# Lookups of expert places moved back in TensorE's order: two spacing numbers of a Fourier-filter and expert-routing kernel

## The chip, the cores and the metric

The kernel runs on one core of a Trainium2 chip. The metric is the device time of one execution in microseconds: 1575.86 us, the median of three runs (1575.03 to 1579.9).

## The reference

Two stages, one behind the other. The first filters 8 sequences of 2496 tokens with 256 channels in the frequency domain. The second routes the 19968 filtered tokens to 8 experts. Each expert takes at most 2496 tokens; the pairs of token and expert are taken in falling order of their score, and a pair whose token is placed or whose expert is full is passed over. Each expert is a two-layer network.

```python
X = np.fft.rfft(x, axis=1)
Y = X * (filt_r + 1j * filt_i)[None, :, :]
x = np.fft.irfft(Y, n=x.shape[1], axis=1).reshape(B * S, D)   # 19968 x 256
cap = N // E                                                  # 2496
flat = (x @ w_gate).flatten()
for idx in np.argsort(-flat):
    tok, e = int(idx) // E, int(idx) % E
    if assigned[tok] >= 0 or counts[e] >= cap:
        continue
    assigned[tok] = e
    counts[e] += 1
for e in range(E):
    mask = assigned == e
    out[mask] = np.maximum(x[mask] @ w1[e], 0.0) @ w2[e]
```

## The kernel before

Up to about 515 us the kernel computes the filter as products with small Fourier matrices and writes the filtered tokens to DRAM (`xs`). From there on it works expert by expert. The greedy assignment is not walked through pair by pair: the kernel finds, eight times, the next expert that fills up, by a search over score thresholds. So experts are numbered 0 to 7 in the order in which they fill up, and while TensorE multiplies for expert e, the search for a later one runs beside it.

**Expert products** (`Ffn.run`). An expert's 2496 rows go in five blocks of 512 (the last of 448). The first layer takes 8 groups of 6 products per block (L872, tile `pz`, 512 or 448 columns; each operand is split into a high and a low part, so three terms). ScalarE takes the positive part (L878) and VectorE the low part of that (L886, for the last block L889, both write `hl`). The second layer takes 24 products per 128 rows (L921, tile `py`, 256 columns). Gathered rows are turned on TensorE (L850) and split by ScalarE (L853) and VectorE (L854). Raw weights are split into high and low parts by ScalarE (L829) and VectorE (L830).

**The search** (`Route.phase`, `threshold`, `counts`). Eleven rounds per expert. In each, VectorE writes a 0/1 mask per token and threshold (`Gm`, L572), TensorE counts with 11 or 13 small products over the rank table `A` (L580), VectorE folds that into `X` (L588 to L590), TensorE sums it over the partitions (L593), and VectorE derives the next thresholds (L617 to L632, `thr` at L610). When the last round is done, a prefix product (L720) gives each partition its first place, and the next expert's preparation runs on VectorE: the maximum over the remaining experts (`M`, L657), two passes over `tmp` (L659, L661), `ar` (L663, L664) and the new rank table `A` (L667). The first count of the next search needs this `A`.

**The lookups** (`Route.places`). They turn the settled assignment into row numbers to gather from (`xid`) and to write to (`oid`). The 2496 places of an expert go in five groups of 512. Per group VectorE makes a one-hot table `OH` (L770, L771), and TensorE looks up two times two blocks of 128 places with it (L777, a pair of products into one PSUM tile `rt`). Behind each pair VectorE takes `loc` (L778), ScalarE two sums (L781), VectorE `ex` (L782); behind the second pair `js`, `xid`, `t1b`, `oid` (L785 to L793). So there are ten pairs per expert. GpSimd then gathers the rows (L836) and later scatters the results (L932). The `rt` tiles of lookups, counts, sums and the prefix product share two PSUM buffers in turn: each waits for the readers of the tile two before it.

**What sets the order.** TensorE's order is written out by hand: `emit` runs through the expert products, and each piece of them advances a clock in class `Pump` by its estimated time (0.65 for three first-layer or six second-layer products, about a microsecond in units of 1). The search and the lookups are generators that yield the kind of their next wait and its length; `Pump.feed` takes their next step when the clock is past its due time. For the lookups the length is taken as it stands: `LO[0]` ahead of the first group, `LO[1]` ahead of the first pair of every later group, `LO[2]` ahead of the second pair of each group, and 3.0 behind a group:

```python
yield 'o', LO[0] if ch == 0 else LO[1]      # L772, OH is issued
...
if t == 0:
    yield 'p', LO[2]                        # L784, between the pairs
...
yield 'g', ch                               # L794, xid and oid are issued
```

One lookup step is taken at most per piece of product. The search waits until the first group of the lookups under way is done (`Pump.first`). If a gather needs a group that the clock hasn't reached, `Pump.until` takes the missing steps at once, with no products between. The other engines' orders are set by a scheduler that plays the program through in time when it is built, so they shift with TensorE's. SP's queue carries loads of the first stage only; GpSimd's carries the gathers, scatters and weight loads.

Of the kernel before, what the change touches and what calls it, by code (L numbers as in the profile page):

```python
# [19 lines left out]
NPOST = 6  # L20

LAGS = [(1.6, 1.2), (1.9, 1.2), (2.4, 1.4), (2.2, 1.3), (2.2, 1.2), (2.6, 1.2), (2.6, 1.2), (2.6, 1.2)]
LO, M0, M1, M7 = (4.2, 1.2, 1.4), 3.5, 4.9, 6.9
TU0, TU, PACE = 1.1, 1.15, 5
ORD, TF = (1, 0, 0, 1), (3, 5)
I1, C0, EZ = 5, -2, 0.8
# [1120 lines left out]
```

## Time and profile before

| | |
|---|---|
| median of three runs | 1575.86 us |
| the profiled execution | 1576.41 us |
| its span, first to last instruction | 1574.5 us |
| TensorE busy: products, weight loads | 90%, 79% |
| VectorE, ScalarE, GpSimd busy | 62%, 46%, 36% |
| mean granted TensorE clock | 0.971 of 2.4 GHz |
| prefix products (L720), start | 497.3, 637.8, 767.0, 892.0, 1011.6, 1133.0, 1249.8, 1276.8 us |

Products on TensorE overlap their neighbours, so their rate is read from the distance of starts. A wait is shown as idle time ahead of an instruction, with the one that ended it last. The granted clock has two levels, 1.2 and 2.4 GHz; a share between 0.5 and 1 in a stretch is a mixture of the two.

### The profile page before, as it was taken

Reading aid. Unit: us, or ns where it says so; the run is one execution under the profiler, and the core shown is the slowest. Engines: PE = TensorE matmul, PEld = TensorE weight load, DVE = VectorE, ACT = ScalarE, POOL = GpSimd, SP = SyncE. Lnnn points to the kernel's source line nnn. Section 1 sums busy time; section 2 is a strip of 40 time slices with the busy share of each in tenths; the row PEclk is TensorE's granted clock in tenths of the full one; section 3 lists DMA queues with packets and bytes.
Section 4 is the critical chain, followed back from the end, with each engine's and each line's share of the span. In section 5 each row is a group of like instructions: output and inputs, shape, how many; then the busy total and the mean of one; then the engine's idle time right before and its main releaser. Section 6 shows DMA issues by size and latency. Waiting matters only on the chain.

```text
span 1574.5 us, 27463 instructions
## 1 busy us (share of the span) xinstructions
PE 1416.7 (90%) x10354; PEld 1237.7 (79%) x10354; DVE 983.8 (62%) x2611; ACT 718.8 (46%) x1703; POOL 564.0 (36%) x566
## 2 busy tenths in 40 slices
PE   0478889999899689989999999999999999999998
PEld 0478888886654478878888888888879889899898
DVE  1558878765656646966786686787686772622322
ACT  1455666663356532633552553453462453632322
POOL 0124544432310253354253344343533443333311
PEclk9989999999999789999999999999999999999999
DMA  9998978447889410211221211211211221111100
GB/s 147 159 120 131 131 133 134 99 134 220 237 280 356 130 52 28 84 57 33 78 66 36 75 44 53 76 51 43 92 42 40 93 98 44 45 44 44 44 28 26
DMA packets 117992, 150.61 MB, mean 96 GB/s; under 512 B 72525, under 2 KB 95651, under 8 KB 115555
## 3 DMA queue, kind: packets, MB, share of 16 engines
q1 hardware_dynamic: 70900, 45.23, 17.1%
q0 software_dynamic: 17840, 60.34, 11.8%
q10 hardware_dynamic: 29119, 43.28, 9.4%
q8 instruction: 82, 1.34, 0.4%
q14 instruction: 51, 0.42, 0.1%
HBM read 85.13 MB, written 63.70 MB: 95 GB/s over the span
## 4 chain that ended last, share of the span: by engine, by line
PE 56%; DVE 14%; DMA 12%; issue 8%; ACT 4%; SPq 2%; POOL 2%; ACTq 1%; another core or an unknown queue 0%; POOLq 0%; DVEq 0%
PE py L921 21%; PE pz L872 20%; DMA xt<-x 6%; PE pv L409 4%; DMA zd<-zt 3%; PE rt L580 2%; DVE xr L211 2%; PE ptr L850 2%; PE p L238 2%; PE pa L293 2%; PE p L223 2%; ACT lg L740 1%; DVE hl L886 1%; POOL out L932 1%; DMA wr<-moe_w,widx 1%
## 5 line engine op out<-in xcount | busy, mean ns | idle before, releaser
L921 PE MATMUL py<-w1h,hl 128*128 128x256 f32 x2496 | 485.8, 287 | 2.0 <-DVE hl L889 1.4
L921 PEld LDWEIGHTS py<-w1h,hl 128*128 128x128 f32 x2496 | 403.5, 192 | 5.5 <-DVE hl L889 2.2
L921 PE MATMUL py<-w1l,hl 128*128 128x256 f32 (+1 forms) x1280 | 360.1, 283 | 0.0
L932 POOL DMA_INDIRECT out<-y,oid x160 | 174.3, 1090 | 452.0 <-ACT y L931 411.9
L878 ACT ACTIVATE hl<-pz 128x512 fp32r<-128x512 f32 (+1 forms) x320 | 187.0, 589 | 224.0 <-PE pz L872 183.2
L872 PE MATMUL pz<-xo,w0h 128*128 128x512 f32 (+1 forms) x640 | 266.9, 417 | 12.1 <-DVE hl L886 6.2
L872 PE MATMUL pz<-z,w0h 128*128 128x512 f32 (+1 forms) x640 | 250.4, 391 | 1.5 <-DVE z L854 1.3
L872 PE MATMUL pz<-xo,w0l 128*128 128x512 f32 (+1 forms) x640 | 251.2, 392 | 0.0
L921 PEld LDWEIGHTS py<-w1l,hl 128*128 128x128 f32 (+1 forms) x1280 | 242.5, 189 | 2.0
L886 DVE SCALAR_TENSOR_TENSOR hl<-pz,hl 128x512 fp32r<-128x512 f32 x227 | 154.8, 687 | 126.0 <-ACT hl L878 123.5
L836 POOL DMA_INDIRECT xg<-xs,xid x160 | 171.1, 1069 | 140.2 <-PE ptr L850 45.9
L931 ACT COPY y<-py 128x256 f32<-128x256 f32 x152 | 56.3, 371 | 294.9 <-PE py L921 255.1
L223 PE MATMUL p<-cS,xr 117*128 117x120 f32 x688 | 97.5, 288 | 64.9 <-ACT xr L211 49.1
L872 PEld LDWEIGHTS pz<-xo,w0h 128*128 128x128 f32 x640 | 123.6, 193 | 33.5 <-DVE hl L886 8.5
L223 PEld LDWEIGHTS p<-cS,xr 117*128 117x128 f32 x688 | 88.9, 202 | 70.3 <-ACT xr L211 49.1
L872 PEld LDWEIGHTS pz<-xo,w0l 128*128 128x128 f32 x640 | 122.1, 191 | 24.3
L872 PEld LDWEIGHTS pz<-z,w0h 128*128 128x128 f32 x640 | 123.0, 192 | 18.1 <-DVE z L854 2.6
L231 ACT COPY Y<-p 64x240 f32<-64x240 f32 (+1 forms) x304 | 116.3, 382 | 25.1 <-PE p L223 15.3
L246 POOL TENSOR_TENSOR P<-P 128x256 f32<-128x256 f32 x80 | 62.3, 780 | 162.7 <-DVE P L244 162.6
L572 DVE TENSOR_TENSOR Gm<-M,thr 117x1232 bf16<-117x1232 f32 (+2 forms) x80 | 104.4, 1315 | 0.2
L238 PE MATMUL p<-cW,Y 128*128 128x128 f32 x640 | 91.3, 284 | 10.6 <-DVE Q L245 7.2
L238 PEld LDWEIGHTS p<-cW,Y 128*128 128x128 f32 x640 | 82.3, 197 | 17.1 <-issue 9.1
(230 smaller groups left out, 2260.7 us busy)
## 6 DMA issues: line engine op xcount, KB each, us to landing
zd<-zt ACTq DMA_DIRECT2D x80, 256.0 KB
xt<-x SPq DMA_DIRECT2D x42, 344.0 KB
z<-zd SPq DMA_DIRECT2D x18, 600.0 KB
xs<-xo ACTq DMA_DIRECT2D x18, 600.0 KB
xt<-zd SPq DMA_DIRECT2D x8, 600.0 KB
xs<-xt ACTq DMA_DIRECT2D x8, 600.0 KB
xs<-Y ACTq DMA_DIRECT2D x6, 600.0 KB
xt<-x SPq DMA_DIRECT2D x147, 21.5 KB
```

The lines of the kernel that those rows point to most:

```text
L223: s.lastmm = nc.tensor.matmul(p[:, q-q0, :120], xv[:, q-24*h], s.cS1, start=True, stop=True).ins
L231: (nc.vector.tensor_copy if t in ((5,) if b else (1, 3, 5, 7, 9)) else nc.scalar.copy)(dst, src)
L238: nc.tensor.matmul(p[:, k], s.Y1[b][:, 4*g+k, dh*128:dh*128+128], s.cW[:, 4*g+k], start=True, stop=True)
L246: nc.gpsimd.tensor_tensor(P[:, :, :64], P[:, :, :64], P[:, :, 64:], op=OP.subtract)
L409: nc.tensor.matmul(p[:120, :w], s.cD, z[:, g-g0:g-g0+w], start=True, stop=True)
L572: nc.vector.tensor_tensor(Gm[:, s0:s1, :m], s.M[:, s0:s1].unsqueeze(2).to_broadcast([117, s1 - s0, m]), thr[:117].unsqueeze(1).to_broadcas ...
L836: s.lastg = s.nc.gpsimd.indirect_dma_start(out=xg[:n], out_offset=None, in_=s.xs, in_offset=bass.IndirectOffsetOnAxis(ap=ids[0][:n, t:t+1] ...
L872: nc.tensor.matmul(p[:, :n], w[:, sl], x[:, k, :n], start=m == 0, stop=m == 5)
L878: s.lasta = nc.scalar.activation(h[:, :n], p[:, :n], AF.Relu).ins
L886: nc.vector.scalar_tensor_tensor(l[:, :n], p[:, :n], 0.0, h[:, :n].bitcast(F32), op0=OP.max, op1=OP.subtract)
L921: nc.tensor.matmul(p[:a.stop-a.start], hs[g][f][:, a], b[:, 256*f:256*f+256], start=m == 0, stop=m == 8 * len(terms) - 1, skip_group_check ...
L932: st = nc.gpsimd.indirect_dma_start(out=out_rows, out_offset=bass.IndirectOffsetOnAxis(ap=ids[1][:w, 4*g+t:4*g+t+1], axis=0), in_=y[:w], i ...
```

## The change

`LO[1]` goes from 1.2 to 2.0 and `LO[2]` from 1.4 to 2.2. (`M0`, `M1` and `M7` stay.)

```diff
-LO, M0, M1, M7 = (4.2, 1.2, 1.4), 3.5, 4.9, 6.9
+LO, M0, M1, M7 = (4.2, 2.0, 2.2), 3.5, 4.9, 6.9
```

All instructions stay; TensorE, VectorE, ScalarE and GpSimd get another order, SP keeps its own. From the prefix product to the first count of the next search stood seven pairs of lookups for experts 1 to 3 and eight for 4 and 5; now it is six for each.

On TensorE, ahead of the first count (`Gm`, L580) behind expert 3's lookups. Names are tiles with their buffer numbers, `pz` the first-layer result and `OH` the one-hot table. Before:

```order
L872 MATMUL pz_10495<-xo_10135,w0l_8477 128x448
L777 LDWEIGHTS OH_10480
L777 MATMUL rt_10502<-tab1_3992,OH_10480 128x180
L777 LDWEIGHTS OH_10480
L777 MATMUL rt_10502<-tab1_3992,OH_10480 128x180
L872 MATMUL pz_10513<-xo_10135,w0h_8476 128x448
L872 MATMUL pz_10513<-z_10136,w0h_8476 128x448
L872 MATMUL pz_10513<-xo_10135,w0l_8477 128x448
L872 MATMUL pz_10513<-xo_10135,w0h_8476 128x448
L872 MATMUL pz_10513<-z_10136,w0h_8476 128x448
L872 MATMUL pz_10513<-xo_10135,w0l_8477 128x448
L580 LDWEIGHTS Gm_3966
```

And now:

```order
L872 MATMUL pz_10498<-z_10134,w0h_8476 128x448
L872 MATMUL pz_10498<-xo_10133,w0l_8477 128x448
L872 MATMUL pz_10511<-xo_10133,w0h_8476 128x448
L872 MATMUL pz_10511<-z_10134,w0h_8476 128x448
L872 MATMUL pz_10511<-xo_10133,w0l_8477 128x448
L872 MATMUL pz_10511<-xo_10133,w0h_8476 128x448
L872 MATMUL pz_10511<-z_10134,w0h_8476 128x448
L872 MATMUL pz_10511<-xo_10133,w0l_8477 128x448
L872 MATMUL pz_10522<-xo_10133,w0h_8476 128x448
L872 MATMUL pz_10522<-z_10134,w0h_8476 128x448
L872 MATMUL pz_10522<-xo_10133,w0l_8477 128x448
L580 LDWEIGHTS Gm_3966
```

The seventh lookup pair stood six products ahead of the count and has gone behind it; the sixth is now fifteen products ahead.

On VectorE at the same place, the rows up to the rank table `A` (L667) that this count reads. Before:

```order
L664 SCALAR_TENSOR_TENSOR ar_3996<-asg_3969,ar_3996 117x176
L778 TENSOR_TENSOR loc_10115<-sidx_3985,rt_10502 128x2
L889 SCALAR_TENSOR_TENSOR hl_10509<-pz_10495,hl_10509 128x64
L889 SCALAR_TENSOR_TENSOR hl_10509<-pz_10495,hl_10509 128x384
L786 SCALAR_TENSOR_TENSOR xid_10092<-ex_10114,js_10116 128x4
L789 TENSOR_TENSOR t7_10118<-js_10116,row_3950 128x28
L792 TENSOR_TENSOR t2_10374<-js_10116,ex_10114 128x4
L889 SCALAR_TENSOR_TENSOR hl_10537<-pz_10513,hl_10537 128x64
L889 SCALAR_TENSOR_TENSOR hl_10537<-pz_10513,hl_10537 128x384
L667 TENSOR_TENSOR A_3965<-ar_3996,row_3950 117x704
```

And now:

```order
L664 SCALAR_TENSOR_TENSOR ar_3996<-asg_3969,ar_3996 117x176
L778 TENSOR_TENSOR loc_10117<-sidx_3985,rt_10479 128x2
L771 SCALAR_TENSOR_TENSOR OH_10737<-iota_3984,BC_10115,oa_10738 117x512
L889 SCALAR_TENSOR_TENSOR hl_10494<-pz_10472,hl_10494 128x64
L889 SCALAR_TENSOR_TENSOR hl_10494<-pz_10472,hl_10494 128x384
L791 TENSOR_REDUCE t1b_10119<-t7_10120 128x4
L830 TENSOR_TENSOR w1l_10108<-wr1_10104,w1h_10107 128x512
L667 TENSOR_TENSOR A_3965<-ar_3996,row_3950 117x704
```

`A` stood behind the split of `pz_10513`, the last products ahead of the count on TensorE; it now stands behind that of `pz_10472`, the one ahead of `pz_10498` in TensorE's order.

On TensorE, ahead of the second count behind expert 2's lookups. Before, the last rows are products alone; now:

```order
L872 MATMUL pz_9130<-xo_8932,w0l_8477 128x512
L850 MATMUL ptr_9140<-id_5112,xg_9028 128x128 x2
L850 MATMUL ptr_9140<-id_5112,xg_9030 128x128 x2
L872 MATMUL pz_9155<-xo_8932,w0h_8476 128x512
L872 MATMUL pz_9155<-z_8933,w0h_8476 128x512
L872 MATMUL pz_9155<-xo_8932,w0l_8477 128x512
L777 LDWEIGHTS OH_9118
L777 MATMUL rt_9159<-tab0_3991,OH_9118 128x180
L777 LDWEIGHTS OH_9118
L777 MATMUL rt_9159<-tab0_3991,OH_9118 128x180
L580 LDWEIGHTS Gm_3966
L580 MATMUL rt_9166<-A_3965,Gm_3966 128x80
```

And before:

```order
L872 MATMUL pz_9140<-xo_8958,w0h_8476 128x512
L872 MATMUL pz_9140<-z_8959,w0h_8476 128x512
L872 MATMUL pz_9140<-xo_8958,w0l_8477 128x512
L872 MATMUL pz_9150<-xo_8958,w0h_8476 128x512
L872 MATMUL pz_9150<-z_8959,w0h_8476 128x512
L872 MATMUL pz_9150<-xo_8958,w0l_8477 128x512
L872 MATMUL pz_9150<-xo_8958,w0h_8476 128x512
L872 MATMUL pz_9150<-z_8959,w0h_8476 128x512
L872 MATMUL pz_9150<-xo_8958,w0l_8477 128x512
L580 LDWEIGHTS Gm_3966
L580 MATMUL rt_9157<-A_3965,Gm_3966 128x80
```

A lookup pair, the ninth of ten, now stands directly ahead of this count.

## Rows read from the trace of the kernel before

**Rows 1.** The page's busy time, share of the span and instructions, by engine.

```profile
PE 1416.7 (90%) x10354; PEld 1237.7 (79%) x10354; DVE 983.8 (62%) x2611; ACT 718.8 (46%) x1703; POOL 564.0 (36%) x566
```

**Rows 2.** TensorE's waits, 637 to 1300 us: total, times, longest, in us.

```profile
PE rt L580 <- DVE Gm L572: 5.4, 2, 4.0
...
PE rt L593 <- DVE X L590: 1.9, 4, 0.7
```

**Rows 3.** Busy us of engines by stretch (PE, PEld, DVE, ACT, POOL), clock, DMA.

```profile
645.00:675.00 30.00, 27.04 (x196) 24.97 (x194) 28.17 (x86) 18.61 (x53) 16.52 (x13) 1.00 0.20 63
777.00:805.00 28.00, 25.64 (x178) 23.84 (x177) 27.23 (x87) 16.98 (x49) 15.62 (x12) 0.97 0.17 53
902.00:930.00 28.00, 24.54 (x164) 21.89 (x163) 26.62 (x83) 17.27 (x51) 14.09 (x12) 0.99 0.19 57
1023.00:1053.00 30.00, 27.34 (x179) 23.62 (x178) 27.90 (x83) 19.42 (x54) 15.67 (x13) 1.00 0.16 49
1141.00:1169.00 28.00, 26.13 (x171) 22.75 (x170) 26.94 (x79) 18.13 (x54) 9.06 (x9) 1.00 0.14 43
...
805.00:820.00 15.00, 14.88 (x114) 12.77 (x114) 7.88 (x35) 5.81 (x19) 8.00 (x9) 0.94 0.25 75
...
1053.00:1064.00 11.00, 10.77 (x99) 10.19 (x100) 6.63 (x42) 4.44 (x16) 2.56 (x3) 1.00 0.15 50
```

**Rows 4.** Timeline of TensorE at its waits: start, us, what, [idle before <-releaser].

```profile
565.77 0.48 PE L777 MATMUL rt<-tab,OH 117*128 117x180 f16 x2 [1.07 <-DVE ex L782]
...
687.51 0.66 PE L580 MATMUL rt<-A,Gm 117*128 117x96 bf16 x6 [3.98 <-DVE Gm L572]
...
795.35 0.33 PE L777 MATMUL rt<-tab,OH 117*128 117x180 f16 x2 [0.92 <-DVE ex L782]
...
917.92 0.33 PE L777 MATMUL rt<-tab,OH 117*128 117x180 f16 x2 [0.47 <-DVE a L751]
...
930.32 0.48 PE L580 MATMUL rt<-A,Gm 117*48 117x64 bf16 x6 [3.31 <-DVE t1b L791]
...
1053.23 0.45 PE L580 MATMUL rt<-A,Gm 117*48 117x48 bf16 x11 [2.01 <-DVE ex L782]
...
1159.04 0.33 PE L777 MATMUL rt<-tab,OH 117*128 117x180 f16 x2 [1.38 <-DVE ex L782]
```

**Rows 5.** Timeline of TensorE, an undisturbed group of lookups.

```profile
1259.41 0.33 PE L777 MATMUL rt<-tab,OH 117*128 117x180 f16 x2
...
1261.64 0.28 PE L921 MATMUL py<-w1h,hl 128*128 128x256 f32 x1
1261.76 0.33 PE L777 MATMUL rt<-tab,OH 117*128 117x180 f16 x2
1261.88 0.36 PE L921 MATMUL py<-w1h,hl 128*128 128x256 f32 x1
```

**Rows 6.** Timeline of VectorE ahead of 687.51, and of TensorE at 692.

```profile
685.42 0.69 DVE L886 SCALAR_TENSOR_TENSOR hl<-pz,hl 128x512 fp32r<-128x512 f32 x1 [3.08 <-ACT hl L878]
686.03 1.43 DVE L572 TENSOR_TENSOR Gm<-M,thr 117x1232 bf16<-117x1232 f32 x1
...
692.63 0.40 PE L872 MATMUL pz<-z,w0h 128*128 128x512 f32 x1
692.86 0.39 PE L872 MATMUL pz<-xo,w0l 128*128 128x512 f32 x1
```

**Rows 7.** VectorE's groups, 902 to 930 us: count, busy us, mean ns, idle before.

```profile
L778 DVE TENSOR_TENSOR loc<-sidx,rt 128x2 f32<-128x2 f32 x7 | 1.0, 146 | 0.0
L782 DVE TENSOR_SCALAR ex<-rt 128x4 f32<-128x4 f32 x6 | 0.9, 152 | 0.0
```

**Rows 8.** Busy time by stretch as in rows 3, around low clock.

```profile
803.00:807.00 4.00, 4.00 (x29) 3.67 (x27) 2.45 (x16) 1.37 (x5) 2.91 (x3) 0.57 0.26 79
...
929.00:936.00 7.00, 5.68 (x26) 4.50 (x27) 3.94 (x21) 2.12 (x9) 0.00 (x0) 0.55 0.01 2
```

**Rows 9.** Timeline of TensorE, first count behind expert 0's lookups.

```profile
560.62 0.31 PE L580 MATMUL rt<-A,Gm 117*48 117x112 bf16 x3 [1.05 <-issue]
```

## The prediction, made before the changed kernel ran

> **What bounds the kernel now.** Three views were read, from coarse to fine: the busy shares of the span, TensorE's waits, then the busy time of each engine stretch by stretch. In the shares TensorE leads: 90% of the span for products, 79% for weight loads, VectorE 62% [rows 1]. So the kernel is paced by TensorE, and a change of order can win only what TensorE still idles. Its waits between 637 and 1300 us name VectorE behind nearly all of them: first of all the masks of the counts (5.4 us), and the sums of the counts with 1.9 us in four places [rows 2]. The stretches show where. Each time an expert's rank is settled, there are some 30 us in which VectorE has the lookups, the new maximum, the new rank table A and the splits of the next weights to do together. In the five of these stretches VectorE is busy 28.17 of 30, 27.23 of 28, 26.62 of 28, 27.90 of 30 and 26.94 of 28 us, and TensorE, over the same stretches, 27.04, 25.64, 24.54, 27.34 and 26.13: it idles 2.96 + 2.36 + 3.46 + 2.66 + 1.87 = 13.3 us there [rows 3]. Right behind them VectorE has room: 7.1 us free of 15 (805 to 820), 4.4 of 11 (1053 to 1064) [rows 3]. VectorE is the bound of these stretches and of nothing else.
>
> The single waits say which step is late [rows 4]. Lookups wait 1.07, 0.92, 0.47 and 1.38 us (565.77, 795.35, 917.92, 1159.04), three of them for ex, the last reader of a PSUM buffer. The first count after A waits 3.31 and 2.01 us (930.32, 1053.23). The 3.98 us at 687.51 is of another kind: its mask stood behind a split of hidden rows that itself waited 3.08 us for ScalarE [rows 4, 6].
>
> **The change part by part.** Nothing is computed more or less. Two numbers move lookups back in TensorE's order: 0.8 more of the order's clock ahead of a group's first lookup and 0.8 between the two of a group.
>
> *Between lookups.* Two lookups of a group stand 2.35 us apart today where nothing waits (1259.41 to 1261.76) [rows 5]. The order now mostly puts three more first-layer products or six more second-layer ones between them. A first-layer product takes 0.23 us from start to start (692.63 to 692.86), a second-layer one 0.12 (1261.64 to 1261.76) [rows 5, 6], so this is 3 x 0.23 = 0.69 or 6 x 0.12 = 0.72 us. From one group to the next it is about 1.2 us more. The waits of 0.47 and 1.38 us stand ahead of a first lookup, the other two ahead of a second one: of 3.84 us some 3.1 is covered.
>
> *Up to the first count.* In a stretch that VectorE bounds the gain isn't the sum of the waits that go, since TensorE would only arrive earlier at the next one. It is what is put on TensorE's side ahead of the first count plus what is taken from VectorE there. Counted in the order from the prefix product (L720) to the first count (L580), for experts 1 to 5: first-layer products 45, 69, 72, 66, 66 become 48, 69, 81, 60, 75; second-layer ones 184, 132, 120, 132, 132 become 184, 138, 114, 156, 120; the turns of gathered rows stay, but for four more, at about 0.12 each, in the fifth. That is 3 x 0.23 = 0.69; 6 x 0.12 = 0.72; 9 x 0.23 - 6 x 0.12 = 1.35; 24 x 0.12 - 6 x 0.23 = 1.50; 9 x 0.23 - 12 x 0.12 + 4 x 0.12 = 1.11; together 5.4 us. Seven pairs of lookup products leave these stretches, 0.12 us a pair (1261.76 to 1261.88 [rows 5]), 0.8 us, so TensorE has 4.6 us more there. From VectorE go four loc of 34 and nine ex of 30, at 0.146 and 0.152 us [rows 7]: 2.0 us. Relief: **6.6 us**, of 13.3 us idle.
>
> *The rank table A.* The second reason to trust this is the third expert's stretch, where the first count waits 3.31 us [rows 4]. In VectorE's order of before A stands behind the split of the very last first-layer products ahead of that count (hl from pz_10513), so no product at all covers the way from TensorE over ScalarE and VectorE back. In the new order the last split ahead of A is that of pz_10472, and fifteen products, 15 x 0.23 = 3.4 us or a little less (they are narrower there), stand between that and the count. The same holds in less measure for the fourth expert, whose count follows a lookup directly today and now has thirty second-layer products in front.
>
> *The clock.* Behind two of these stretches the granted clock falls to its lower level: a mean of 0.55 over 929 to 936 us and of 0.57 over 803 to 807 [rows 8]. Products run at that share of their rate there, which costs (1 - 0.55) x 7 = 3.2 and (1 - 0.57) x 4 = 1.7 us. The first follows the 3.31 us wait, the second a run of short waits. Bounds: nothing, if the shorter waits still bring it down; 4.9 us if both go. I take **2.0**, since another wait of this size, 2.01 us at 1053.23, cost no clock (1.00 over 1053 to 1064 [rows 3, 4]): which wait brings it down is partly luck.
>
> *Expert 0.* Its lookups are forced together at the start, as before. One more is forced now: the second lookup of group 2 stands 1.2 us behind the first instead of 2.1, because a gather needs its places. It uses another buffer than the first, so it needn't wait; if it does, the rows bound it by the longest lookup wait, 1.38 us. The wait of 1.07 us at 565.77 gets some 0.7 us more cover: **0.7**. The counts just ahead of it lose about 3.3 us in gaps that nothing on the page explains (1.05 at 560.62 is one [rows 9]); they may stay or go, and stand in the range only.
>
> *What is pushed back.* Thirteen of the fifty lookup pairs of experts 1 to 5 stand behind the first count today, twenty will. There they meet the counting rounds, whose sums already wait, 0.5 us each [rows 2]. Seven more pairs beside them: nothing if the 4 to 7 us that VectorE has free take them, 7 x 0.5 = 3.5 us if each holds up a sum. I take **1.3**, nearer the lower end by the free time of [rows 3]. Later gathers cost nothing: in the order each group's indices are still asked for nine or more units of its clock (about a microsecond each) after they are made, except in expert 0. ScalarE's two sums per lookup move along and ScalarE is at 46% [rows 1]. The search as a whole ends 1 to 3 us later per expert; between that point, where the next weights are sent for, and the next expert's first product lie 28 units or more, and the last expert's lookups stay far ahead of the end, so no tail grows.
>
> Sum: 6.6 + 2.0 + 0.7 - 1.3 = **8.0 us**. The profiled execution took 1576.41 us (span 1574.5 and 1.9 around it), 0.55 above the median of 1575.86. 1576.4 - 8.0 = 1568.4, or, as a median, **1568**.
>
> **The rivals.**
>
> *The wait moves on.* VectorE's work per expert is the same, and what the first count no longer waits for, the masks and sums of the next rounds do. For it: waits on masks and sums of 5.4 and 1.9 us exist already [rows 2]. Against: 4 to 7 us free right behind [rows 3]. If six of the eight microseconds come back: 1574.
>
> *VectorE isn't the bound.* With 62% over the span it has 600 us to spare, and who goes by that figure expects nothing: 1576. The windows speak against it, with 93 to 97% in the stretches concerned [rows 1, 3]. The Trainium skill has this reading: its page "Perfetto Trace Analysis", section "Identifying the Most-Contended Engine", tells to take the engine of highest occupancy first, and TensorE by its weight loads; by that rule this change, which leaves TensorE's work alone, does nothing. The same page's section "Optimization Strategy" allows that the most contended engine changes between regimes, and by that rule the trace agrees with the forecast.
>
> *Slower: masks behind lookups.* Five of the pushed lookup pairs now stand directly ahead of a count, with no product between. If that count's mask (1.43 us [rows 6]) stood in VectorE's order behind the pair's loc (0.15 us [rows 7]), TensorE would wait for lookup, loc and mask: about 0.3 + 0.15 + 1.43 = 1.9 us. At all seven more pairs that is 13 us, less the gain 5 us slower, with a clock fall of 1.7 us 1582 to 1583. It decides from five of the seven on. Against it: the order of VectorE has the masks ahead of these loc, and where loc comes first three or more us of products lie between pair and count; only in expert 0 it is 2.2.
>
> That the change doesn't do what it says can be ruled out but for the one forced lookup.
>
> **How the numbers follow.** Forecast 0.65 (1568, own range 1560 to 1573), the wait moves on 0.18 (1574), VectorE not the bound 0.06 (1576), slower 0.11 (1582). 0.3% is 4.7 us, about what can be told from no change: faster is below 1571.1, slower above 1580.6. Of the forecast's own chance 0.05 lies above 1571.1. So faster 0.60, within 0.29, slower 0.11. The range reaches down to where the first counts' and lookups' waits, both clock falls and the odd gaps all go, 1576 - 17 = 1559, and up to 1578, which leaves out the slower rival and little else.
>
> **What would show it.** In the five stretches from prefix product to first count TensorE's idle time falls from 13 to some 6 or 7 us, with VectorE still above 90%; lookups wait under 1 us in all; no first count waits 3 us, and the clock stays at 1.00 there. Wrong would be: idle time of the stretches as before; or as much new idle time in the 20 us behind the first counts, on L580 or L593, with loc (L778) or ex (L782) as releaser. A gain that lies in expert 0, or ahead of the first lookup, isn't this mechanism.

## The result and the profile after

The changed kernel takes **1564.72 us** (median of 4, 1560.57 to 1568.96), the kernel before, in the same set of runs, 1577.88 (median of 4). The ratio is **0.9923, 95% interval 0.9896 to 0.9951**: 12 us less, 8 to 16 by the interval. The prediction was 1568 in a range of 1559 to 1578, with 0.60 on faster. The profiled execution took 1568.96 us (span 1567.1), 7.4 us less than the profiled one of before: the two profiles show some 7 of the 12 us.

All instructions are as many as before and about as long. The page's busy line, against [rows 1]:

```profile
PE 1420.3 (91%) x10354; PEld 1243.2 (79%) x10354; DVE 989.7 (63%) x2611; ACT 718.7 (46%) x1703; POOL 561.3 (36%) x566
```

TensorE's waits from 637 to 1300 us (total, times, longest), against [rows 2]:

```profile
PE rt L580 <- DVE ex L782: 8.1, 3, 4.0
PE rt L593 <- DVE X L590: 3.4, 5, 2.4
PE pz L872 <- DVE hl L889: 2.5, 2, 1.5
```

No lookup (L777) waits any more; the masks (`Gm`, L572) are gone from the list too. In their place three counts wait for `ex`, the last reading of a lookup's PSUM buffer. The stretches from the first lookup to the first count, for experts 1 to 5, against [rows 3] (stretch, its length, busy us and instructions of PE, PEld, DVE, ACT, POOL, then granted clock, DMA share, GB/s):

```profile
645.00:674.00 29.00, 27.36 (x200) 25.49 (x198) 26.84 (x81) 17.11 (x49) 14.80 (x12) 1.00 0.15 46
778.00:806.00 28.00, 26.35 (x188) 24.36 (x186) 27.05 (x81) 16.71 (x48) 12.15 (x11) 1.00 0.15 46
902.00:930.00 28.00, 25.86 (x174) 23.04 (x173) 27.39 (x81) 17.96 (x49) 14.70 (x11) 1.00 0.15 49
1017.00:1047.00 30.00, 28.02 (x194) 24.72 (x193) 28.22 (x82) 17.77 (x49) 12.99 (x12) 1.00 0.16 49
1135.00:1163.00 28.00, 27.81 (x182) 24.19 (x181) 27.27 (x73) 19.03 (x51) 15.36 (x11) 1.00 0.16 48
```

TensorE idles 1.64 + 1.65 + 2.14 + 1.98 + 0.19 = 7.6 us there, where it idled 13.3; VectorE is at 93 to 98%. For all kernels alike, the rest of this text uses the whole way from prefix product (L720) to first count (L580) of these five searches, and the 20 us behind each first count. The sums over the five, before and after, each pair of lines in this order:

```profile
sum 192.20, PE 173.23 PEld 154.32 DVE 176.56 ACT 123.40 POOL 80.71; mean PE 34.65 PEld 30.86 DVE 35.31 ACT 24.68 POOL 16.14
sum 100.00, PE 95.08 PEld 82.62 DVE 63.97 ACT 39.61 POOL 41.54; mean PE 19.02 PEld 16.52 DVE 12.79 ACT 7.92 POOL 8.31
```

```profile
sum 186.20, PE 176.60 PEld 157.57 DVE 172.79 ACT 119.46 POOL 78.23; mean PE 35.32 PEld 31.51 DVE 34.56 ACT 23.89 POOL 15.65
sum 100.00, PE 90.02 PEld 78.35 DVE 64.22 ACT 37.75 POOL 46.93; mean PE 18.00 PEld 15.67 DVE 12.84 ACT 7.55 POOL 9.39
```

Up to the first count TensorE's idle time falls from 192.20 - 173.23 = 19.0 to 186.20 - 176.60 = 9.6 us; behind it it rises from 4.9 to 10.0. In this pair of profiles half of the relief comes back at once. The new waits, in TensorE's timeline (start, us, what, idle before and its releaser):

```profile
686.15 1.06 PE L580 MATMUL rt<-A,Gm 117*128 117x96 bf16 x11 [3.96 <-DVE ex L782]
...
929.85 0.50 PE L580 MATMUL rt<-A,Gm 117*48 117x64 bf16 x11 [2.14 <-DVE ex L782]
...
1051.18 0.17 PE L593 MATMUL rt<-X,ones 128*128 128x9 f16 x1 [2.45 <-DVE X L590]
...
1172.20 0.44 PE L580 MATMUL rt<-A,Gm 117*128 117x32 bf16 x11 [2.04 <-DVE ex L782]
```

The second is expert 3's first count, which waited 3.31 us in [rows 4]; the first stands at nearly the same place of the program as the 3.98 us there.

### The profile page after: what moved, and what is told of

Same layout as the page of the kernel before. It is cut to its first block, busy times and chain, and to the rows that moved or that the text cites. A ratio compares the mean times of both kernels' runs of the same rounds, so it can differ in the third digit from the quotient of the medians.

```text
span 1567.1 us, 27445 instructions
## 1 busy us (share of the span) xinstructions
PE 1420.3 (91%) x10354; PEld 1243.2 (79%) x10354; DVE 989.7 (63%) x2611; ACT 718.7 (46%) x1703; POOL 561.3 (36%) x566
## 5 line engine op out<-in xcount | busy, mean ns | idle before, releaser
L836 POOL DMA_INDIRECT xg<-xs,xid x160 | 174.3, 1089 | 146.5 <-issue 72.0
L223 PE MATMUL p<-cS,xr 117*128 117x120 f32 x688 | 101.9, 296 | 63.2 <-ACT xr L211 51.3
L223 PEld LDWEIGHTS p<-cS,xr 117*128 117x128 f32 x688 | 93.0, 209 | 69.0 <-ACT xr L211 51.3
L231 ACT COPY Y<-p 64x240 f32<-64x240 f32 (+1 forms) x304 | 116.0, 382 | 27.5 <-PE p L223 14.3
L572 DVE TENSOR_TENSOR Gm<-M,thr 117x1232 bf16<-117x1232 f32 (+2 forms) x80 | 106.5, 1342 | 0.2
```

The lines of the kernel that those rows point to most:

```text
L223: s.lastmm = nc.tensor.matmul(p[:, q-q0, :120], xv[:, q-24*h], s.cS1, start=True, stop=True).ins
L231: (nc.vector.tensor_copy if t in ((5,) if b else (1, 3, 5, 7, 9)) else nc.scalar.copy)(dst, src)
L572: nc.vector.tensor_tensor(Gm[:, s0:s1, :m], s.M[:, s0:s1].unsqueeze(2).to_broadcast([117, s1 - s0, m]), thr[:117].unsqueeze(1).to_broadcas ...
L836: s.lastg = s.nc.gpsimd.indirect_dma_start(out=xg[:n], out_offset=None, in_=s.xs, in_offset=bass.IndirectOffsetOnAxis(ap=ids[0][:n, t:t+1] ...
```

## The experiments

Ten more kernels, the changed kernel again and the kernel before again ran in three sets, each set beside the kernel before on a chip of its own (the record numbers them 7, 0 and 10; for the result above it has no number). The kernel before took 1554.5 and 1555.5 us in the first and third set and 1577.7 in the second. So times are compared within a set, and profiles of the second set with the two above, whose times are like it. Idle times are TensorE's, in us, worked out from a sum line of windows as above, one profile each.

| kernel | set | us | ratio to before, 95% | idle to the first count | idle in the 20 us behind |
|---|---|---|---|---|---|
| before (another profile) | 3 | (1545.99, one run) | | 17.0 | 0.0 |
| the changed kernel again | 3 | 1542.24 | 0.9919 (0.9901 to 0.9937) | 9.7 | 2.4 |
| half: between groups | 1 | 1553.58 | 1.0004 (0.9982 to 1.0025) | 14.3 | 3.3 |
| half: inside a group | 1 | 1542.67 | 0.9931 (0.9910 to 0.9952) | 10.5 | 2.0 |
| whole train later | 1 | 1543.85 | 0.9935 (0.9913 to 0.9957) | 13.9 | 0.1 |
| late output rows | 1 | 1554.82 | 1.0005 (0.9986 to 1.0024) | 15.0 | 0.0 |
| later prefix product, 0.3 | 3 | 1547.66 | 0.9952 (0.9934 to 0.9969) | 13.5 | 0.5 |
| `ex` first | 3 | 1545.07 | 0.9947 (0.9923 to 0.9971) | 10.1 | 2.2 |
| later maximum | 2 | 1571.96 | 0.9963 (0.9942 to 0.9985) | 18.6 | 3.3 |
| later prefix product, 0.8 | 2 | 1571.79 | 0.9952 (0.9933 to 0.9971) | 11.4 | 10.5 |
| twice inside a group | 2 | 1580.68 | 1.0004 (0.9980 to 1.0028) | 12.8 | 15.2 |
| one operation more per pair | 2 | 1578.86 | 0.9997 (0.9978 to 1.0017) | 20.3 | 5.6 |

**The two halves, and the train as a whole.** Three edits of one line of the kernel before:

```diff
-LO, M0, M1, M7 = (4.2, 1.2, 1.4), 3.5, 4.9, 6.9
+LO, M0, M1, M7 = (4.2, 2.0, 1.4), 3.5, 4.9, 6.9
```

> Half of the change alone: 0.8 more ahead of a group's first lookup, the spacing inside a group as before. In the order the products between prefix product and first count stay as they were before the change (34.4, 33.2, 32.9, 33.0, 33.5 us of TensorE work for experts 1 to 5, against 34.6, 33.4, 33.1, 33.4, 33.8 before and 35.1, 33.9, 34.3, 34.5, 34.6 after), while seven lookup pairs leave these stretches. Theory 1 (TensorE needs more products ahead of the first count, because VectorE bounds the stretch): only VectorE's 2.0 us less 0.8 us of lookups, so 1 to 2 us faster, 1574 to 1575 beside a before of 1576. Theory 2 (the gain is in the lookups' own waits): the two waits ahead of first lookups go, 1.9 us faster, and the rest of the gain belongs to the other half. Theory 3 (any new order of TensorE lands somewhere within some 10 us by luck of what meets what): any value, with no relation to these numbers.

```diff
-LO, M0, M1, M7 = (4.2, 1.2, 1.4), 3.5, 4.9, 6.9
+LO, M0, M1, M7 = (4.2, 1.2, 2.2), 3.5, 4.9, 6.9
```

> The other half alone: 0.8 more between the two lookups of a group. The products between prefix product and first count are those of the full change (35.3, 34.1, 34.5, 34.7, 34.7 us), the lookups there 70 matmuls instead of 74. Theory 1: most of the gain of the full change, 6 to 10 us faster. Theory 2: the two waits ahead of second lookups go, about 2 us faster. Theory 3: any value.

```diff
-LO, M0, M1, M7 = (4.2, 1.2, 1.4), 3.5, 4.9, 6.9
+LO, M0, M1, M7 = (5.0, 1.2, 1.4), 3.5, 4.9, 6.9
```

> No more room between lookups; the whole train of lookups starts 0.8 later (5.0 instead of 4.2 ahead of the first). Products between prefix product and first count come out nearly as in the full change (35.3, 34.6, 34.4, 34.2, 34.9 us, 5.1 us more than before in all), the spacing is that of before. Theory 1: 5 to 9 us faster, like the full change. Theory 2: nothing, within 2 us, since lookups stand as close as before. Theory 3: any value.

The half between groups is worth nothing (+0.6 us, -2.8 to +3.9), although it takes seven lookup pairs out of the stretches. The half inside a group is worth 10.7 us (7.5 to 14), the later train 10.1 (6.7 to 13.5), both a little above what theory 1 had for them. The later train has the lookups as close together as before, so **room between lookups isn't what pays**; theory 2 falls. What the two have in common stands in the pump: the next search may only go on once the first group's second lookup is out. Both put 0.8 units in front of that point, so 0.8 units more of products stand between prefix product and first count, and every later prefix product moves back. The half between groups touches neither.

**VectorE's load.** Two tries. The first makes the output rows of experts 2 to 5 once instead of group by group (parts of the edit are left out at the dots):

```diff
-            nc.vector.tensor_tensor(t7, js[:, ts].unsqueeze(2).to_broadcast([128, 4, 7]),
-                                    s.k22.unsqueeze(1).to_broadcast([128, 4, 7]), op=OP.is_ge)
...
+            if not 1 < ph < 6 or ch == 4:
+                cs, w = (ts, 4) if not 1 < ph < 6 else (slice(0, 20), 20)
...
+                nc.vector.tensor_tensor(t7, js[:, cs].unsqueeze(2).to_broadcast([128, w, 7]),
```

> TensorE's order is that of the kernel before, instruction by instruction. For experts 2 to 5 the four VectorE operations that make the output rows of a group (0.178 + 0.175 + 0.154 + 0.159 = 0.67 us) are done once, for all five groups, behind the fifth: VectorE has three to four groups' worth, 2.0 to 2.7 us, less ahead of each of four first counts, 8 to 10 us in all. Theory 1 (VectorE's load bounds these stretches): 4 to 8 us faster with TensorE's order untouched. Theory 2 (waits of lookups): 0 to 1 us. Theory 3 (luck of TensorE's order): nothing, since that order is unchanged.

No gain (+0.8 us, -2.2 to +3.7). The dose was smaller than I had priced it: the sums over the five stretches, of before (from the third set) and of this kernel, show VectorE only 3.0 us less busy.

```profile
sum 187.90, PE 170.86 PEld 152.50 DVE 175.95 ACT 122.45 POOL 80.18; mean PE 34.17 PEld 30.50 DVE 35.19 ACT 24.49 POOL 16.04
```

```profile
sum 188.50, PE 173.50 PEld 153.39 DVE 172.93 ACT 123.14 POOL 78.77; mean PE 34.70 PEld 30.68 DVE 34.59 ACT 24.63 POOL 15.75
```

Durations of small operations overlap: in one profile `ex`, `js` and the rank table start at 914.10, 914.16 and 914.23 us, though `ex` is shown with 0.16 us. So their 0.15 to 0.18 us are not what each takes of VectorE's time. The stretches didn't become shorter, 188.5 against 187.9 us: TensorE idles 2.0 us less there, but is busy for 2.6 us more. One of them has a fall of the clock inside, (1 - 0.67) x 5 = 1.7 us:

```profile
757.00:762.00 5.00, 4.76 (x14) 3.74 (x15) 4.89 (x18) 1.78 (x4) 0.00 (x0) 0.67 0.67 267
```

Without it they would be some 1.1 us shorter, for 3.0 us less work, and by the interval of the times the kernel is at most 2.2 us faster. So a part of the load removed may have paid, not all of it; more can't be told from this run.

The second try added an operation per pair:

```diff
                 nc.vector.tensor_scalar(ex[:, u], pr[:, :, S+1:S+3], MID, None, op0=OP.add)
+                if ph:
+                    nc.vector.tensor_scalar(v("jk", [117, 512], F16, bufs=1), s.iota, 1.0, None, op0=OP.mult)
```

> The order of before with one VectorE operation more per lookup pair (117x512 fp16, about 0.35 us by the like operation of the masks of the places), whose result nothing reads: 3.5 us more of VectorE work per expert, some 2.5 us of it ahead of each first count, 12 us ahead of the five. Theory 1 in the form that VectorE's throughput bounds these stretches: 8 to 14 us slower. If only the order of a few dependent steps binds there and VectorE has room between them, as the late output rows (no gain from 8 us less) suggest: 0 to 4 us slower.

It **failed as an experiment**. The group's row (durations, first and last start) shows that all seventy started by 521.1 us, over 100 us ahead of the second expert's lookups, the first that they were meant for; nothing in the kernel tied them to the lookups:

```profile
L784 DVE TENSOR_SCALAR jk<-iota x70: 267/286/335, 479.8 to 521.1; 117x512 f16<-117x512 f16 x70
```

It is a repeat of the kernel before, and looks like it: 20.3 us of idle time to the first counts, 5.6 behind.

**Cover put elsewhere, and a larger dose.**

```diff
-            yield 'd', 5.5
+            yield 'd', 6.3
```

> The lookups keep the numbers of before; instead the step behind which the next rank table is worked out (the wait ahead of the new maximum's use, 5.5 units of the order's clock) is made 0.8 longer. Products between prefix product and first count rise by 0.5 to 1.4 us per expert (32.4, 31.7, 30.9, 31.0, 31.0 to 33.8, 32.5, 32.2, 31.9, 31.5 us), and every later prefix product moves back as in the full change. Lookups stand at most where they stood. Theory 1 (it is the cover ahead of the first count, wherever it is put, that pays): 6 to 11 us faster, as the second half of the change and the shifted train were. Theory 2 (room between and ahead of lookups pays): nothing, within 2 us. Theory 4 (what pays is where the prefix products of later experts fall among first- and second-layer products): 6 to 11 us as well; the next run tells it from theory 1.

5.8 us faster (2.4 to 9.2), but not by the way of theory 1: idle time up to the first counts stays, 18.6 against 19.0 us. TensorE does 180.92 us of work there instead of 173.23, and the stretches grew by as much, from 192.2 to 199.5 us. So more products ahead of the count did not lower TensorE's idle time by themselves; why isn't shown. Four of the five first counts wait, three of them 1.1 to 1.6 us for `ex` or `loc` of a lookup and one 2.80 us without a releaser. The 5.8 us are about the lower end of what theory 4 had; one profile doesn't show where they are.

```diff
-LO, M0, M1, M7 = (4.2, 1.2, 1.4), 3.5, 4.9, 6.9
+LO, M0, M1, M7 = (4.2, 1.2, 3.0), 3.5, 4.9, 6.9
```

> Twice the second half of the change: 1.6 more between the two lookups of a group, nothing more ahead of groups. Between prefix product and first count 33.8, 33.2, 33.0, 33.3, 32.9 us of products (the single dose had 33.1, 32.4, 32.3, 32.5, 31.6, before 32.4, 31.7, 30.9, 31.0, 31.0). Theory 1: the first counts of experts 2 to 5 still waited 1.5 us in one place with the single dose, so 1 to 3 us more than it, 11 to 14 us faster than before in all. Theory 2: no more than the single dose, whose lookups wait for nothing. Theory 4: any value between before and 14 us faster.

Not faster than before at all. Idle time up to the first counts is still low, 12.8 us, but 15.2 us stand behind them. The longest of these, with what VectorE did ahead of it:

```profile
688.45 0.25 DVE L588 TENSOR_TENSOR t<-rt,row 48x96 f32<-48x96 f32 x1 [4.87 <-remote]
...
689.71 0.20 PE L593 MATMUL rt<-X,ones 128*128 128x18 f16 x1 [6.44 <-DVE loc L778]
```

The stall on VectorE has no releaser that the profile knows ("remote"). So this run shows that the gain ends, but not whether by the dose or by such stalls.

**Where the prefix product falls.** Two kernels move the prefix products and leave the numbers of lookups and rank table alone:

```diff
-LO, M0, M1, M7 = (4.2, 1.2, 1.4), 3.5, 4.9, 6.9
+LO, M0, M1, M7 = (4.2, 1.2, 1.4), 3.5, 5.7, 6.9
```

> Lookups and rank table keep the numbers of before; the wait ahead of the prefix product is 0.8 longer (5.7 instead of 4.9 units). Later prefix products move back by 1.4, 2.8, 4.3, 5.6, 7.1, 8.5 us in the order's product time, more than in the full change, but between prefix product and first count only 0.3 us more stands per expert (32.4, 31.8, 31.6, 31.8, 31.5). Theory 1 (cover ahead of the first count): 1 to 2 us faster. Theory 4 (place of the prefix products): the waits 2.4 and 9.8 us behind the prefix products of experts 3, 4 and 6 (1.35, 2.2, 1.4 us) change, some 5 us either way. If VectorE's own wait for the prefix product (3.5 to 3.8 us per expert, which grows by 0.8) is what binds: 4 us slower.

```diff
-LO, M0, M1, M7 = (4.2, 1.2, 1.4), 3.5, 4.9, 6.9
+LO, M0, M1, M7 = (4.2, 1.2, 1.4), 3.5, 5.2, 6.9
```

> Lookups and rank table keep the numbers of before; the wait ahead of the prefix product is 0.3 longer (5.2 instead of 4.9 units), which is the step at which the later prefix products move: those of experts 4, 6 and 7 come to stand behind 144, 216 and 225 finished blocks of the first layer (142, 214 and 223 before; 143, 216 and 225 in the full change). Between prefix product and first count stand as many products as before (31.7, 31.5, 31.1, 30.9 us for experts 2 to 5; 31.7, 30.9, 31.0, 31.0 before; 32.4, 32.3, 32.5, 31.6 in the full change). Theory 4 (the gain is where the prefix products fall): the waits 9.8 us behind that of expert 3 (1.36 us) and 2.4 us behind those of experts 4 and 6 (2.2 and 1.4 us) go, 4 to 6 us faster, while the first counts of experts 3 and 4 wait as before (3.3 and 2.0 us). Theory 1 (cover ahead of the first count): 0 to 1 us faster.

> The changed kernel itself, beside the others on one chip, so that they can be set against it: 8 to 16 us faster than before, as measured. Theory 1: waits ahead of first counts fall; theory 4: the waits 2.4 and 9.8 us behind prefix products are gone.

> The kernel before, for a profile from the same chip as the changed kernel's. All theories: the same time as before. The waits that stand in the profile of before at 9.8 us behind the third expert's prefix product (1.36 us) and at 2.4 us behind the fourth's and sixth's (2.2, 1.4 us), and at the first counts of the third and fourth (3.3, 2.0 us), should be there again if they belong to the order; the 3.98 us at 687.51 and the gaps of expert 0's first counts should not all be, if they belong to the execution.

The first is 7.6 us faster (4.6 to 10.6), more than any theory had for it. The second has hardly more products between prefix product and first count than before, and is 7.5 us faster (4.8 to 10.3): **some 60% of the 12.6 us** that the changed kernel is worth in that set. So most of the gain doesn't need more cover. Whether the remaining 5 us do, or come from the place of the lookups, isn't shown. The first counts of experts 3 and 4 did not wait as before, as theory 4 had them do (more on this below).

What a prefix product's place does is seen at expert 4's, in the profile of before. The rows are ScalarE's eight penalties on the logits (L740), TensorE's prefix product and next first-layer product, and VectorE's splits and its copy of the prefix product (L721):

```profile
1008.34 4.33 ACT L740 ACTIVATE lg<-lg,pen 117x176 f32<-117x176 f32 x8 [0.55 <-DVE pen L709]
...
1011.63 0.17 PE L720 MATMUL rt<-tb,tri 117*117 117x2 f16 x1
...
1012.55 1.09 ACT L878 ACTIVATE hl<-pz 128x512 fp32r<-128x512 f32 x2
1013.26 1.29 DVE L886 SCALAR_TENSOR_TENSOR hl<-pz,hl 128x512 fp32r<-128x512 f32 x2 [3.69 <-ACT hl L878]
...
1014.00 0.50 PE L872 MATMUL pz<-xo,w0h 128*128 128x512 f32 x1 [2.21 <-DVE hl L886]
...
1014.46 0.15 DVE L721 COPY pf<-rt 117x2 f32<-117x2 f32 x1
```

ScalarE is busy for 4.33 us with the penalties. The relus behind them are late, so VectorE's splits wait 3.69 us, TensorE's next product waits 2.21 us for a PSUM buffer, and the copy that the whole search hangs on stands behind two of these splits, 2.8 us after the prefix product. In the changed kernel, one block of products further on:

```profile
1006.46 4.43 ACT L740 ACTIVATE lg<-lg,pen 117x176 f32<-117x176 f32 x8
...
1008.77 0.16 DVE L721 COPY pf<-rt 117x2 f32<-117x2 f32 x1 [1.35 <-PE rt L720]
...
1010.78 1.57 ACT L878 ACTIVATE hl<-pz 128x512 fp32r<-128x512 f32 x3
```

The copy stands ahead of the splits and TensorE doesn't wait. Before has two more waits of first-layer products close behind prefix products: 1.41 us at 1252.19, behind expert 6's and again behind the penalties, and 1.36 us at 901.78, 9.8 us behind expert 3's. The cause of the latter is another: VectorE's split of turned rows (L854), which ends it, stands behind a split of weights (L830). All three were there again in before's second profile (1.35 at expert 3, 1.82 at expert 4, 1.41 at expert 6), as was the wait of the third expert's first count (2.88; the fourth's was 0.97 instead of 2.01), and at none of these places in the changed kernel's two. With the prefix product 0.3 later they are 0.76, 0.63 and nothing. In the list of waits of [rows 2] they are part of lines that the rows leave out, the two at experts 4 and 6 of its second:

```profile
PE pz L872 <- DVE hl L886: 4.8, 5, 2.2
```

The other profiles sort by the same three waits. They stand in the late output rows (1.36, 2.12, 1.43), in the kernel with one operation more (1.35, 2.23, 1.41) and in the half between groups, none of which gained anything. The rows of the last:

```profile
888.45 0.50 PE L872 MATMUL pz<-xo,w0h 128*128 128x512 f32 x1 [1.34 <-DVE z L854]
...
995.76 0.51 PE L872 MATMUL pz<-xo,w0h 128*128 128x512 f32 x1 [1.80 <-DVE hl L886]
...
1228.34 0.50 PE L872 MATMUL pz<-xo,w0h 128*128 128x512 f32 x1 [1.41 <-DVE hl L886]
```

In the half inside a group, the later train and `ex` first none of the three is left. The later prefix product 0.8 has another wait of 0.99 us at expert 6, the later maximum 1.92 us at expert 2 in their place. Twice inside a group has none of the three either, but 1.16 us at expert 2 and 1.00 at expert 6, and no gain: with these waits gone a kernel needn't be faster. That the three waits go was foretold for one kernel, the prefix product 0.3 later; what new waits a place brings was foretold for none, and this much of theory 3 (luck of what meets what) stands.

The first count of expert 3 didn't go by its products either. In before's second profile it waited 2.88 us; with the prefix product 0.3 later, and hardly more products ahead of it (31.5 us of them instead of 30.9), its row shows none. The rows of before, then those of this kernel, with VectorE's rank table ahead of the count:

```profile
907.79 0.67 DVE L889 SCALAR_TENSOR_TENSOR hl<-pz,hl 128x64 fp32r<-128x64 f32 x2
...
908.39 0.87 DVE L667 TENSOR_TENSOR A<-ar,row 117x704 bf16<-117x704 f32 x1
...
909.40 0.48 PE L580 MATMUL rt<-A,Gm 117*48 117x64 bf16 x11 [2.88 <-DVE t1b L791]
```

```profile
914.23 0.89 DVE L667 TENSOR_TENSOR A<-ar,row 117x704 bf16<-117x704 f32 x1
...
915.64 0.50 PE L580 MATMUL rt<-A,Gm 117*48 117x64 bf16 x11
```

Before, the rank table starts 1.9 us after TensorE came to the count (909.40 - 2.88 = 906.52); now 1.4 us ahead of it. Nothing late holds it up in before's second profile: the split ahead of it begins without a wait, and VectorE shows none from 895 us on. It has more to do there: 108 operations from the prefix product to the rank table, in 36.8 us, against 99 in 33.9 us with the prefix product 0.3 later and 97 in 34.6 us in the changed kernel. So at this count VectorE's work ahead of the rank table is what binds; at the first counts of experts 2 and 5 the rank table was done 0.2 and 1.8 us before TensorE came. A part of the wait has moved: with the prefix product 0.3 later a lookup 7 us earlier waits 1.09 us for `ex`.

**Taking ScalarE out of VectorE's line.** On the changed kernel:

```diff
+                nc.vector.tensor_scalar(ex[:, u], pr[:, :, S+1:S+3], MID, None, op0=OP.add)
                 for h in range(2):
                     c = 4*ch + t + h
                     nc.scalar.activation(s.junka, pr[:, h, :S], AF.Sign, bias=loc[:, c:c+1], scale=-1.0, accum_out=js[:, c:c+1])
-                nc.vector.tensor_scalar(ex[:, u], pr[:, :, S+1:S+3], MID, None, op0=OP.add)
```

> The changed kernel, TensorE's order untouched, with VectorE's second reading of a lookup (ex, L782) issued straight behind the first (loc), ahead of ScalarE's two sums instead of behind them: VectorE no longer stands at ex until ScalarE is through (12.7 us of such waits in 80 places in the kernel before). In the changed kernel counts waited 8.1 us in three places for ex. If those waits are VectorE standing in line behind ScalarE: 2 to 5 us faster than the changed kernel. If ScalarE's sums, which read the same PSUM buffer, are what is late: within 1 us of it. If, as the junk operation and the late output rows suggest, VectorE has room enough: within 1 us too.

1545.07 us beside 1542.24 of the changed kernel: no gain. The changed kernel's waits for `ex`, 2.16 us at expert 3's first count and 2.03 us at expert 5's second, are gone. In their place the first counts of experts 3 and 5 wait 1.64 and 1.26 us for the rank table, and a sum of expert 5 waits 1.41 us. No version tried beats the changed kernel.

## Why the prediction was right, point by point

- **The relief of 6.6 us up to the first count: right in size.** In the pair of profiles of the third set, which has none of the stalls told of in the last section, idle time there falls by 17.0 - 9.7 = 7.4 us, in the first pair by 9.4. The steps fit too: TensorE was to have 4.6 us more there, and has 174.83 - 170.86 = 4.0 (3.4 in the first pair); VectorE was to lose 2.0 us, and lost 175.95 - 173.33 = 2.6 (3.8). The sums of the changed kernel in that set:

```profile
sum 184.50, PE 174.83 PEld 156.37 DVE 173.33 ACT 119.57 POOL 76.91; mean PE 34.97 PEld 31.27 DVE 34.67 ACT 23.91 POOL 15.38
```

- **But not by the reasons given alone.** That VectorE's load sets the length of these stretches was argued from 93 to 97% busy; taking 3.0 us of it away brought nothing that can be told, and seven pairs fewer (half of the change) nothing either. VectorE's load was the bound chiefly at one place, the rank table of expert 3; elsewhere what was late hung on a few dependent steps: prefix product, copy, relu and split. The step that failed is the rule behind the sum, that the relief is "what is put on TensorE's side ahead of the first count plus what is taken from VectorE there". The later maximum put 180.92 - 173.23 = 7.7 us more on TensorE's side and 2.6 on VectorE's, and TensorE's idle time there fell by 0.4 instead of 5.1; the prefix product 0.3 later put 1.0 us there, took 1.8 from VectorE, and gained 7.5.
- **What the sum lacked: the prefix products' place.** It counted the kinds of products between prefix product and first count. That the search ends later was seen, but what its end meets there was put at nothing. The prefix product moves by a block, and 1.35 + 1.82 + 1.41 = 4.6 us of waits behind it go. They had stood in the timeline of before, outside the waits that were chosen for [rows 4]. The first two, 3.2 us, are part of the 7.4; the third lies at expert 6, outside the five stretches.
- **The rank table A: half right.** Expert 3's first count waits 2.14 us instead of 3.31; none waits 3 us. But the late split wasn't the cause: in before's second profile that split isn't late, and the count waits 2.88 us. Nor did the fifteen products cover the way. The rank table still starts 0.5 us after TensorE has come to the count (929.85 - 2.14 = 927.71), and `ex`, which ends the wait, stands behind it and a split:

```profile
928.19 0.93 DVE L667 TENSOR_TENSOR A<-ar,row 117x704 bf16<-117x704 f32 x1
...
929.59 0.20 DVE L782 TENSOR_SCALAR ex<-rt 128x4 f32<-128x4 f32 x1
```

- **Lookups' own waits: right.** 3.84 us became none (before's second profile has 2.7 of them, the changed kernel's none).
- **The clock, 2.0 us: not shown.** The fall behind expert 3 is smaller and the one at 803 us is gone, but one stands behind the new wait at 1172 (against [rows 8]; the clock is the third number from the end):

```profile
929.00:936.00 7.00, 6.16 (x44) 5.90 (x45) 5.78 (x28) 0.85 (x2) 1.89 (x2) 0.76 0.14 42
```

```profile
803.00:807.00 4.00, 3.71 (x36) 3.30 (x35) 3.70 (x15) 2.05 (x9) 3.15 (x3) 1.00 0.23 68
```

```profile
1172.00:1177.00 5.00, 4.80 (x36) 4.71 (x37) 3.32 (x17) 1.35 (x5) 1.01 (x1) 0.66 0.08 26
```

  (1 - 0.76) x 7 + (1 - 0.66) x 5 = 3.4 us against 4.9. Over all ten windows of the sums above, though, nothing is won: by their clocks before loses 0.03 x 38.5 + 0.01 x 38.3 + 0.04 x 41.6 + (0.09 + 0.03 + 0.15) x 20 = 8.6 us, and the changed kernel 0.04 x 39.2 + (0.17 + 0.09 + 0.09) x 20 = 8.6; in the third set it is 1.8 and 3.6. That the clock would stay at 1.00 behind the first counts was wrong. Over the timed runs of the third set the mean granted clock was 0.9766 before and 0.9792 after; 0.0026 x 1545 = 4 us, which may be where part of the gain lies that the profiles don't show.
- **What is pushed back, 1.3 us: too small.** Idle time in the 20 us behind the first counts grew by 5.1 us in the first pair and by 2.3 in the undisturbed one. The piece that both have is the count at 1172.20, directly behind a lookup pair, which waits 2.04 us for `ex` (2.03 in the second profile). That is the price of the slower rival, 1.9 us, at one place instead of five; its reason was another, `ex` behind ScalarE's two sums and not the mask behind `loc`. The 3.96 us at 686.15 and the 2.45 at 1051.18 were 0.30 and nothing in the second profile.
- **Expert 0, 0.7 us: not shown.** The wait of 1.07 us is gone and the odd gaps stayed, but before's second profile has neither at that place. Both belong to the execution, not to the order.
- **The wait moves on** (0.18) was half true in the first pair of profiles, where of 9.4 us 5.1 came back, and less so in the undisturbed one, 2.3 of 7.4. **VectorE not the bound, no change,** is refuted as a forecast: TensorE's work is unchanged and the time fell. By the Trainium skill, page "Perfetto Trace Analysis", section "Optimization Strategy", the most contended engine may change between regimes; the runs agree only in part: the busy share of the stretch found the place, 13.3 us of idle TensorE, but not the cause.

What stays open: from the first prefix product to the end TensorE's idle time fell from 57.0 to 48.2 us in the first pair of profiles and from 44.9 to 37.8 in the second, so they locate 7 to 9 of the 12 us. In the second pair the executions themselves differ by 0.5 us only: that of before took 1545.99 us, less than any of the thirteen others (1548.74 to 1563.53), that of the changed kernel 1545.46, the most of its six. TensorE was busy for 3.8 us more there behind the first prefix product, and that product itself, which no lookup precedes, came 2.8 us later. So a pair of single profiles can't place the rest.

## What to carry to other kernels

Where one engine is almost full for 30 us and another waits for it, look not at its load alone but for the few steps on which the chain hangs, and at what stands ahead of them in its queue. A number that spaces work out often moves everything behind it too: undo the spacing and keep the shift (and the reverse) before believing in either. Price small operations by the distance of their starts, not by their durations.

## What the runs showed of the hardware

The kernel before took 1577.7 us on one chip (number 0) and 1554.5 and 1555.5 on two others (7 and 10), and the profiles differ by stalls without a known releaser ("remote" or "issue"). Behind the first prefix product each profile of the second set, and each of the two of the result, has seven to twelve of over 2.1 us on ScalarE and VectorE; no profile of the first and third set has one. In the profile of the changed kernel that goes with the result ScalarE stood still for 8.55 us and 3.43 us, and VectorE for 4.68; in the third set the same kernel's profile has no such stall:

```profile
564.48 0.37 ACT L931 COPY y<-py 128x256 f32<-128x256 f32 x1 [8.55 <-remote]
...
1050.40 0.20 DVE L588 TENSOR_TENSOR t<-rt,row 48x48 f32<-48x48 f32 x1 [4.68 <-remote]
1050.53 0.37 ACT L931 COPY y<-py 128x256 f32<-128x256 f32 x1 [3.43 <-remote]
```

Of the same sort was the 3.98 us in front of the mask in [rows 4]. The split ahead of that mask waited for a relu of ScalarE, which had stood still itself:

```profile
684.79 0.60 ACT L878 ACTIVATE hl<-pz 128x512 fp32r<-128x512 f32 x1 [3.68 <-remote]
```

In before's second profile the count at that place, expert 1's second, doesn't wait:

```profile
670.78 0.64 PE L580 MATMUL rt<-A,Gm 117*128 117x96 bf16 x11
```

What these stalls are wasn't found. A large wait in one profile is worth a second profile before it is put into a sum.
